# Five prices and waits of a list schedule: loads, stores and two gathers

## The chip, the core and the metric

One core of a Trainium2 chip runs the kernel. Its engines are TensorE (PE in the profile; its weight loads are PEld), VectorE (DVE), ScalarE (ACT) and GpSimd (POOL). SyncE (SP) computes nothing and issues most DMA transfers; GpSimd issues the rest. Each engine takes its instructions in the order in which the program gives them, and waits at the head of that order until the inputs and the buffer of the next one are there. The metric is device time in microseconds (us), the median of runs.

## The reference

The output of windowed attention goes through a routed layer of eight experts and then through a dense layer:

```python
# 2 x 8 heads, 576 tokens, 64 per head; window of 64
scores = where(0 <= i - j < 64, q @ k.T / 8, -1e9)
x = softmax(scores) @ v                     # as 1152 tokens x 512
logits = x @ w_gate                         # 8 experts, the best one per token
gate = softmax(logits)[best]
# tokens of one expert in order, at most 288 each
y[token] = gate * (relu(x[token] @ w1[best]) @ w2[best])   # 512 -> 1024 -> 512
h = y @ w_in                                # 512 -> 2048
out = (h * clip(h + 3, 0, 6) / 6) @ w_out   # 2048 -> 512
```

## The kernel before

**Attention.** The 1152 tokens lie in nine pairs of 64-token groups: pair j holds groups 2j and 2j+1. Per pair SyncE loads rows of q, k and v (`load_rows`, L472), TensorE turns them, and copies on VectorE or ScalarE bring them back from PSUM. `scores` (L564) multiplies, `mask_max` (L580, VectorE, line L587, four instructions) masks a group and finds its maxima, `exps` (L595, ScalarE, L600) takes the exponentials, `p_turn` (L606, TensorE, L610) turns them, `values` (L621, TensorE, L628) multiplies them with v and, in the same matmuls, with v times the gate's weights, so that the logits come along. `finish` (L637, VectorE) divides by the sums and `store_x` (L658, SyncE) stores the pair to DRAM.

**Routing and the early expert.** After five pairs the choice of experts for their tokens is made (`choose`, first row L125). The expert with the most of these tokens is the early expert: its weights are loaded (`early_load`), a gate step on VectorE works out flags and factors, five products on GpSimd (L897) prepare the tokens' index, and `early_gather` (L810) has GpSimd fetch 128 of its rows from DRAM. `early_scale` (L814) multiplies these rows by their gates, on ScalarE (line L468) or VectorE (L464); `early_turn` (L817) turns them, and TensorE starts on that expert. After the last pair `ranks` counts all tokens per expert and sorts the experts; its last line is the cast of the expert list (eofI, L948), from which SyncE takes the addresses of all the other experts' weights. `first_gather` (L965) then fetches the first rows for them.

**What sets the order in the attention.** A list scheduler, `run_nodes` (L430), writes the program. Each step is a node with a priority, the engines that can do it with a cost in us (PE, A, V, P, and D for SyncE's queue), the steps that it needs, the ring of buffers that it takes from, and a lag between its end on the engine and its result. The planner keeps a clock per engine (L406) and takes again and again the ready node with the lowest key

```python
t = max(clock[e], r)
if e == "PE" and t < COLD:
    c = 2 * c
key = (t + EPS * prio + (c if len(engs) > 1 else min(engs.values())) * CW, prio)
```

so a changed cost or lag moves steps on all engines: where a copy can run on ScalarE or VectorE, it also decides on which. Before COLD a TensorE step counts twice its cost.

**What sets it behind the attention.** A second planner writes the experts' stage. It starts from the clocks at which the first one ended (`est.update(clock)`, L1873), and from the planned ends of `rk` (the ranks) and `g0` (the first gather). Weights of an expert arrive in pieces of 512 KB (w1 at L280, w2 at L283) in a ring of buffers (raw); each half of a piece is split into a high part (a cast, L267, mostly on ScalarE) and a low part (L272, VectorE), and TensorE multiplies with both. TensorE's work goes into `fill` (L1263), which puts in front of it whatever job of SyncE, ScalarE, VectorE and GpSimd fits the planned time.

Among these jobs is the conversion of the dense layer's weights, which come as 64-bit numbers. A conversion job (`conv64`, L186; `conv_job`, L1147) loads 512 KB into one of three buffers (raw64, `NR64` = 3; L196 for w_in, L199 for w_out), takes an absolute value on ScalarE (L206), goes through five or six steps on VectorE (L212 to L236; the last one, L236, frees the buffer), and for the first units GpSimd stores the result to DRAM in 256 KB transfers. SyncE has one queue for all of this: an experts' load behind a conversion load leaves after it, even if its own buffer has long been free.

Of the kernel before, what the change touches and what calls it, by code (L numbers as in the profile page):

```python
# [23 lines left out]
def tile_kernel(ctx, tc, q, k, v, w_gate, w1, w2, w_in, w_out, out, cap):  # L24
    nc = tc.nc
    B, H, S, D = q.shape
# [82 lines left out]
    V = nc.vector  # L109
# [8 lines left out]
    def bc(ap, shape):  # L118
        return ap.to_broadcast(shape)
# [201 lines left out]

    NWARM = 9
    GAP = -0.2
    EPS, CW, COLD, LAG = 0.015, 0.3, 6.0, 0.15
    PRIO = {'q': -30, 'k': -29, 'v': -27, 'tq': -7, 'eq': 8, 'tk': -10, 'ek': 3, 'cv': 1, 'tv': 1, 'ev': 2, 'gw': 1, 'ew': 1, 'tw': 1, 'ex': -4, 's': 2, 'm': 5, 'e': 2, 'pt': 2, 'ep': 9, 'av': 2, 'f': 8, 'st': 0, 'top': -5, 'tail': 2, 'ear': 78, 'hot': 60, 'gt': 25, 'fl': 13, 'ga': 58, 'xE': 5, 'turn': 20}
    CS = {'xE': 1.15, 'ep': 1.07, 'eq': 1.07, 'sE': 1.15, 'rk': 1.3, 'q': 1.15, 'v': 0.7}
    with ExitStack() as actx:
# [64 lines left out]
        def rows(t, src, j):  # L392
            o = 0
            while o < 128:
                b, s = divmod(128 * j + o, S)
                n = min(128 - o, S - s)
                yield t[o : o + n, :, 0:D], src[b, :, s : s + n, :].rearrange("h p d -> p h d")
                o += n
# [4 lines left out]
        rings = {'q': 3, 'k': 4, 'v': 3, 'qd': NQD, 't': 2, 's': 2, 'sp': 1, 'p': 1, 'o': 1, 'x': 1, 'neg': 4, 'pe': 3, 'pT': 4, 'vT': 3, 'vw': 4, 'xt': 4}  # L403
        taken = {r: [] for r in rings}
        freed = {}
        clock = dict.fromkeys(("PE", "A", "V", "P", "D"), 0.0)  # L406

        def node(name, prio, engs, fn, needs=(), take=None, free=(), lag=LAG):
            engs = {e: c * CS.get(name[0] if isinstance(name, tuple) else name, 1.0) for e, c in engs.items()}
            nodes[name] = (prio, engs, fn, needs, take, free, lag)  # L410
# [61 lines left out]
        def load_rows(which, j):  # L472
            src, eng = {"q": (q, nc.sync), "k": (k, nc.sync), "v": (v, nc.sync)}[which]

            def run(e):
                box[which, j] = t = ld.tile([128, H, D], F32, name=which + "_sb", bufs=rings[which])
                for o, i in rows(t, src, j):
                    eng.dma_start(o, i)  # L478

            return run  # L480
# [24 lines left out]
        def turn_rows(src, key):  # L505
            def run(e):
                box[key] = pt = quarters(bank("t"))
                t = box[src]
                for hp in range(H // 2):
                    nc.tensor.transpose(  # L510
                        pt[:, hp, :], t[:, 2 * hp : 2 * hp + 2, :].rearrange("p h d -> p (h d)"), ident
                    )

            return run

        def q_out(j):
            def run(e):
                copy(e, qd[j % NQD], box["tq", j], D ** -0.5)

            return run  # L520

        def k_out(j):
            o = 64 * (j + 1)
            return lambda e: copy(
                e, kT[:, :, 0 : 2 * KO].rearrange("p h (a t) -> p h a t", a=2)[:, :, :, o : o + 64],
                box["tk", j].rearrange("p h (a t) -> p h a t", a=2),
            )
# [130 lines left out]
        def store_x(j):  # L658
            xt = box["xt", j]
            nc.sync.dma_start(x_dram[128 * j : 128 * j + 128, :], xt.rearrange("p a h d -> p (a h d)"))  # L660
# [10 lines left out]
        for j in range(NJ):  # L671
            p = 10 * j + (PRIO["tail"] if j == NJ - 1 else 0)
            for nm in ("q", "k", "v"):
                node(("l" + nm, j), p + PRIO[nm], {"D": 1.25}, load_rows(nm, j), take=nm, lag=2.0)
            parts = 3 if j + 1 < NJ else 2
            holders["v", ("lv", j)] = 1 + parts
            node(("tq", j), p + PRIO["tq"], {"PE": 0.44}, turn_rows(("q", j), ("tq", j)), [("lq", j)], "t", [("q", ("lq", j))])
            node(("eq", j), p + PRIO["eq"], {"A": 0.5, "V": 0.6}, q_out(j), [("tq", j)], "qd", [("t", ("tq", j))])
            node(("tk", j), p + PRIO["tk"], {"PE": 0.44}, turn_rows(("k", j), ("tk", j)), [("lk", j)], "t", [("k", ("lk", j))])
            node(("ek", j), p + PRIO["ek"], A_V, k_out(j), [("tk", j)], None, [("t", ("tk", j))])  # L680
            for i in range(parts):
                old = j - NV + (i == 2)
                node(
                    (f"cv{i}", j), p + PRIO["cv"] + i, {"P": 0.6}, v_copy(j, i), [("lv", j)] + [("av", old)] * (old >= 0),
                    None, [("v", ("lv", j))],
                )
            node(("tv", j), p + PRIO["tv"], {"PE": 0.44}, turn_rows(("v", j), ("tv", j)), [("lv", j)], "t", [("v", ("lv", j))])
            node(("ev", j), p + PRIO["ev"], A_V, v_out(j), [("tv", j)], "vT", [("t", ("tv", j))])
            node(("gw", j), p + PRIO["gw"], {"PE": 0.27}, v_gate(j), [("ev", j), "wg"], "x", [("vT", ("ev", j))])
            node(("ew", j), p + PRIO["ew"], {"A": 0.16, "V": 0.2}, w_out_(j), [("gw", j)], "vw", [("x", ("gw", j))])  # L690
            node(("tw", j), p + PRIO["tw"], {"PE": 0.11}, w_turn(j), [("ew", j)], "x", [("vw", ("ew", j))])
            old = [("av", i) for i in (j - NV, j - NV + 1) if i >= 0]
            node(("ex", j), p + PRIO["ex"], {"A": 0.32, "V": 0.4}, x_out(j), [("tw", j)] + old, None, [("x", ("tw", j))])
            for g in (2 * j, 2 * j + 1):
                o = p + g % 2
                if g % 2 == 0:
                    needs = [("eq", j), ("ek", j)] + [("ek", j - 1)] * (j > 0)
                    node(("s", j), o + PRIO["s"], {"PE": 0.93}, scores(j), needs, "sp", [("qd", ("eq", j))])
                    holders["sp", ("s", j)] = 2
                node(("m", g), o + PRIO["m"], {"V": 0.84}, mask_max(g), [("s", j)], "neg", [("sp", ("s", j))])  # L700
                node(("e", g), o + PRIO["e"], {"A": 1.17}, exps(g), [("m", g)], "pe", [("neg", ("m", g))])
                tp = "p" if g + 1 < NG else "t"
                node(("pt", g), o + PRIO["pt"], {"PE": 0.44}, p_turn(g), [("e", g)], tp, [("pe", ("e", g))])
                node(("ep", g), o + PRIO["ep"], A_V, p_out(g), [("pt", g)], "pT", [(tp, ("pt", g))])
            free = [("pT", ("ep", 2 * j)), ("pT", ("ep", 2 * j + 1))]
            needs = [("ep", 2 * j), ("ep", 2 * j + 1), ("ex", j), ("cv0", j), ("cv1", j)]
            if j:
                needs += [("ex", j - 1), ("cv2", j - 1)]
            node(("av", j), p + PRIO["av"], {"PE": 1.15}, values(j), needs, "o", free)
            if j + 1 < NJ:  # L710
                node(("f", j), p + PRIO["f"], {"V": 1.3}, lambda e, j=j: finish(j), [("av", j)], "xt", [("o", ("av", j))])
                node(("st", j), p + PRIO["st"], {"D": 0.62}, lambda e, j=j: store_x(j), [("f", j)], None, [("xt", ("f", j))])
            else:
                node(("f", j), p + PRIO["f"], {"V": 0.85}, lambda e, j=j: finish(j), [("av", j)])


        p = 10 * NE + PRIO["top"]
# [104 lines left out]
        def early_load(u, h):  # L822
            def run(e):
                if "eE" not in box:
                    box["eE"] = nc.sync.value_load(eI[0:1, 0:1], min_val=0, max_val=E - 1)
                weights_in(wE[2 * u + h], box["eE"], u, h)

            return run
# [55 lines left out]
        node("gE", p + PRIO["fl"], {"V": 1.35}, early_gate, ["fl"])  # L884
        node("ix", p + PRIO["fl"], {"PE": 0.2}, early_index, ["gE"], "x")
        node("ie", p + PRIO["fl"], {"V": 0.3}, early_index_out, ["ix"], None, [("x", "ix")])
        node("ga", p + PRIO["ga"], {"P": 1.04}, early_gather, ["ie"], lag=3.0)
        node("sE", p + PRIO["turn"], {"A": 0.48, "V": 0.4}, early_scale, ["ga"])
        node("tE", p + PRIO["turn"], {"PE": 0.44}, early_turn, ["sE"], "x")
        node(  # L890
# [3 lines left out]
        for j in range(NE):  # L894
            node(
                ("hotp", j), p + PRIO["hot"], {"P": 0.36},
                lambda e, j=j: nc.gpsimd.tensor_tensor(  # L897
                    out=A1t[:, j], in0=A1[:, j], in1=bc(c_tok[:, j : j + 1], [128, 128]), op=ALU.mult
                ),
                ["gE"],  # L900
            )
        for u in range(NFU):
            for h in range(2):
                node(("wl", u, h), p + 2 * u + h, {"D": 1.3}, early_load(u, h), ["pl"], lag=2.0)
        for u in range(NEU):
            o = p + PRIO["ear"] + 2 * u
            node(("e0", u), o, {"PE": 0.86}, early_up(u, 0), ["xE", ("wl", u, 0)], "s")
# [88 lines left out]
        p = -100  # L996
# [4 lines left out]
        node("sa", p, {"V": 1.4}, slots, ["rk"], None, [("t", "cn")])  # L1001
        node("px", p, {"PE": 0.25}, slot_index, ["sa"] + [("hotp", j) for j in range(NE)], "t")
        node("sx", p, {"V": 0.1}, lambda e: V.tensor_copy(sidx, box["ix"][:, 0:NA]), ["px"], None, [("t", "px")])
        node("g0", p, {"P": 1.04}, first_gather, ["sx"], lag=3.0)
        node("gt", PRIO["gt"], {"V": 0.9}, gate_parts, ["ch"])
        node("gc", PRIO["gt"], {"V": 0.6}, gate_columns, ["gt", "px"])
        for j in range(NE, NJ):
# [46 lines left out]
    for n, (small, b) in enumerate(TEAMS):  # L1054
        at_ = dict.fromkeys("abw", 0)
        order = ORDER[n]
        for c in order:
            f = at_[c]
# [795 lines left out]
    for g, (small, b) in enumerate(TEAMS):  # L1854
        st = start[False, small[0]]
# [134 lines left out]
```

## Time and profile before

| what | before |
|---|---|
| median of 3 runs | 445.79 us |
| lowest to highest | 444.71 to 446.35 us |
| the profiled execution's own time | 445.48 us |
| its span in the trace | 443.7 us |
| mean granted clock of TensorE | 0.983 |
| TensorE busy | 410.0 us, 92% |
| VectorE busy | 322.7 us, 73% |
| ScalarE busy | 224.8 us, 51% |
| GpSimd busy | 56.7 us, 13% |

The trace covers the span; 1.8 us of the profiled execution's time lie outside it. Attention and routing take the first 75 us or so; the experts follow, from 238 us on mixed with the dense layer (the first ScalarE step of its gate, L1556, starts at 237.5), which fills the rest. Shares over the whole span say little of one stage, so the prediction reads single stretches: a table by stage (busy time, granted clock and DMA share in a stretch), the chain of waits (followed back from the last instruction, each step to what released it) and timelines of one engine (when each instruction started, and in brackets how long the engine had been idle and for whom).

### The profile page before, as it was taken

What the parts mean: (1) busy time and instruction counts of PE and PEld (TensorE: products, weight loads), DVE (VectorE), ACT (ScalarE), POOL (GpSimd) and SP (SyncE); (2) the same over time, 40 slices, a digit from 0 to 9 for tenths busy, and PEclk for the clock granted to TensorE, in tenths of its full rate; (3) what the DMA queues carried; (4) which work ended last, traced back from release to release, by engine and by line L of the source; (5) the groups of instructions that cost most, each with busy time, mean ns of one, the idle gap of its engine ahead of it and who ended that gap; (6) DMA issues with size and microseconds to landing.
All of it is one profiled execution on the core that took longest, in us unless ns stands there. A gap on an engine that the chain in (4) does not pass through costs nothing.

```text
span 443.7 us, 8561 instructions
## 1 busy us (share of the span) xinstructions
PE 410.0 (92%) x3055; PEld 348.2 (78%) x3055; DVE 322.7 (73%) x867; ACT 224.8 (51%) x492; POOL 56.7 (13%) x120
## 2 busy tenths in 40 slices
PE   7999867699698999999899999999999999999992
PEld 4887654488587898987689998888888888998981
DVE  2888937779799999979777999999999422222430
ACT  4886733572458877735468453455553222322330
POOL 8632401203002002010000000000000000110111
PEclk9999989999899999999899999999999999999997
DMA  9996943996999999569975323442410000110101
GB/s 173 202 234 159 323 153 114 341 338 199 369 338 364 328 324 353 169 171 381 354 234 192 100 90 100 139 124 71 134 55 0 1 0 0 49 47 1 47 28 51
DMA packets 68883, 75.99 MB, mean 171 GB/s; under 512 B 31104, under 2 KB 49536, under 8 KB 68832
## 3 DMA queue, kind: packets, MB, share of 16 engines
q1 hardware_dynamic: 66288, 67.13, 49.6%
q0 software_dynamic: 2544, 8.23, 4.9%
q8 instruction: 26, 0.43, 0.4%
q14 instruction: 25, 0.20, 0.2%
HBM read 67.49 MB, written 7.86 MB: 170 GB/s over the span
## 4 chain that ended last, share of the span: by engine, by line
PE 64%; DVE 14%; DMA 13%; ACT 3%; issue 3%; SPq 2%; POOL 0%; POOLq 0%; DVEq 0%; ACTq 0%
PE banks L253 54%; DMA raw<-in_moe_w_dram 9%; DVE wt L272 5%; PE banks L628 2%; PE banks L510 2%; DMA c<-x_dram,eI 2%; PE banks L610 1%; ACT wt L267 1%; DMA v_sb<-in_v_dram 1%; SPq L478 1%; PE banks L574 1%; PE banks L1495 1%; DMA out_dram<-part,cidx 1%; DVE neg L587 1%; DVE raw L221 1%
## 5 line engine op out<-in xcount | busy, mean ns | idle before, releaser
L253 PE MATMUL banks<-x,wt 128*128 128x320 f32 (+3 forms) x576 | 107.2, 336 | 0.5 <-ACT x L1386 0.4
L253 PEld LDWEIGHTS banks<-x,wt 128*128 128x128 f32 x576 | 94.3, 188 | 10.7 <-DVE wt L272 0.7
L253 PE MATMUL banks<-wt,g 128*128 128x512 f32 x384 | 92.8, 390 | 0.0
L272 DVE TENSOR_TENSOR wt<-raw,wt 128x512 fp32r<-128x512 f32 x128 | 82.5, 684 | 11.6 <-ACT wt L267 10.7
L267 ACT CAST wt<-raw 128x512 fp32r<-128x512 f32 x128 | 75.3, 621 | 30.7 <-DMA raw<-in_moe_w_dram 21.1
L253 PEld LDWEIGHTS banks<-wt,g 128*128 128x128 f32 x384 | 71.6, 188 | 14.2
L1556 ACT ACTIVATE r<-banks,c_three 128x320 f32<-128x320 f32 (+3 forms) x48 | 27.9, 581 | 70.3 <-PE banks L253 70.3
L1559 DVE SCALAR_TENSOR_TENSOR gf<-r,banks 128x320 f32<-128x320 f32 (+3 forms) x48 | 26.5, 552 | 47.7 <-ACT r L1556 47.3
L253 PE MATMUL banks<-xT,wt 128*128 128x256 f32 (+2 forms) x288 | 39.9, 286 | 2.3 <-ACT wt L267 1.5
L253 PEld LDWEIGHTS banks<-xT,wt 128*128 128x128 f32 x288 | 35.7, 194 | 4.8 <-ACT wt L267 2.3
L253 PE MATMUL banks<-h,wt 128*128 128x256 f32 (+2 forms) x288 | 37.0, 279 | 0.0
L253 PEld LDWEIGHTS banks<-h,wt 128*128 128x128 f32 x288 | 34.6, 191 | 0.5 <-issue 0.5
L1562 ACT CAST g<-gf 128x320 fp32r<-128x320 f32 (+2 forms) x40 | 21.4, 536 | 21.0 <-DVE gf L1559 20.8
L1565 DVE TENSOR_TENSOR g<-gf,g 128x320 fp32r<-128x320 f32 (+2 forms) x40 | 23.3, 582 | 9.5 <-ACT g L1562 9.1
L253 PE MATMUL banks<-wt,xT 128*128 128x256 f32 x144 | 22.8, 305 | 4.8 <-ACT wt L267 3.4
L206 ACT ACTIVATE c<-raw 128x512 f32<-128x512 f32 x32 | 21.5, 675 | 10.6 <-DVE t L230 10.1
L253 PEld LDWEIGHTS banks<-wt,xT 128*128 128x128 f32 x144 | 19.8, 201 | 7.6 <-ACT wt L267 4.6
L1602 POOL DMA_INDIRECT out_dram<-raw,cidx x4 | 4.0, 988 | 160.7 <-issue 158.1
L587 DVE CUSTOM_DVE_ANT_0 neg<-banks,tmask 128x128 f32<-128x128 f32 x72 | 16.3, 284 | 8.7 <-PE banks L574 8.7
L600 ACT ACTIVATE pe<-neg,nmx 128x128 f32<-128x128 f32 x72 | 22.4, 392 | 0.1
L230 DVE SCALAR_TENSOR_TENSOR t<-raw,c 128x512 f32<-128x512 uint32 x32 | 22.0, 687 | 0.7 <-DMA wd_dram<-t 0.2
L221 DVE SCALAR_TENSOR_TENSOR raw<-raw,c 128x512 uint32<-128x512 uint32 x32 | 22.0, 687 | 0.3
(286 smaller groups left out, 568.2 us busy)
## 6 DMA issues: line engine op xcount, KB each, us to landing
raw<-in_moe_w_dram SPq DMA_DIRECT2D x64, 512.0 KB
raw<-in_moe_w_in_dram SPq DMA_DIRECT2D x16, 512.0 KB
raw<-in_moe_w_out_dram SPq DMA_DIRECT2D x16, 512.0 KB
early<-in_moe_w_dram SPq DMA_DIRECT2D x8, 512.0 KB
wd_dram<-t POOLq DMA_DIRECT2D x12, 256.0 KB, 5.9
raw<-wd_dram SPq DMA_DIRECT2D x6, 512.0 KB
x_dram<-xt SPq DMA_DIRECT2D x9, 256.0 KB
q_sb<-in_q_dram SPq DMA_DIRECT2D x8, 256.0 KB
```

Of the source, the lines that this page charges most:

```text
L206: nc.scalar.activation(box["c"].bitcast(F32), box["hi"].bitcast(F32), AF.Abs)
L221: nc.vector.scalar_tensor_tensor(out=a.bitcast(U32), in0=box["hi"], scalar=0xC0000000, in1=box["c"], op0=ALU.bitwise_and, op1=ALU.bitwise_or,)
L230: nc.vector.scalar_tensor_tensor(out=box["t"], in0=box["lo"], scalar=2.0 ** -52, in1=box["c"].bitcast(F32), op0=ALU.mult, op1=ALU.mult)
L253: nc.tensor.matmul(out, l, r, start=(start and n == 0), stop=(stop and n == len(pairs) - 1))
L267: nc.scalar.copy(hi, r)
L272: V.tensor_tensor(out=lo, in0=r, in1=hi.bitcast(F32), op=ALU.subtract)
L587: V.tensor_tensor_reduce(out=neg[:, hp, :], in0=box["sp", g][:, hp, :], in1=tmask[:, first, :], scale=-1.0, scalar=3.0e38, op0=ALU.add, op ...
L600: nc.scalar.activation(pe[:, hp, :], neg[:, hp, :], AF.Exp, bias=nmx[:, hp : hp + 1], scale=-1.0)
L1556: nc.scalar.activation(r, ph, AF.Relu, bias=c_three)
L1559: V.scalar_tensor_tensor(out=gf, in0=r, scalar=6.0, in1=ph, op0=ALU.min, op1=ALU.mult)
L1562: nc.scalar.copy(hi, gf)
L1565: V.tensor_tensor(out=lo, in0=gf, in1=hi.bitcast(F32), op=ALU.subtract)
```

## The change

Seven numbers of the two planners' inputs are changed, all in the attention's list schedule. A load of q, k, v counts 1.46 us of SyncE's queue in place of 1.25, a store of a pair 0.73 in place of 0.62, a load of the early expert's weights 1.46 in place of 1.3. The queue's clock starts at 2.4 in place of 0, and TensorE's steps count double until 8.4 in place of 6.0. The early expert's gather counts as landed 6 us after its issue in place of 3, the first gather of the experts' stage 5 in place of 3.

```diff
@@ -321,7 +321,7 @@
-    EPS, CW, COLD, LAG = 0.015, 0.3, 6.0, 0.15
+    EPS, CW, COLD, LAG = 0.015, 0.3, 8.4, 0.15
@@ -403,7 +403,7 @@
-        clock = dict.fromkeys(("PE", "A", "V", "P", "D"), 0.0)
+        clock = dict.fromkeys(("PE", "A", "V", "P"), 0.0) | {"D": 2.4}
@@ -671,7 +671,7 @@
-                node(("l" + nm, j), p + PRIO[nm], {"D": 1.25}, load_rows(nm, j), take=nm, lag=2.0)
+                node(("l" + nm, j), p + PRIO[nm], {"D": 1.46}, load_rows(nm, j), take=nm, lag=2.0)
@@ -709,7 +709,7 @@
-                node(("st", j), p + PRIO["st"], {"D": 0.62}, lambda e, j=j: store_x(j), [("f", j)], None, [("xt", ("f", j))])
+                node(("st", j), p + PRIO["st"], {"D": 0.73}, lambda e, j=j: store_x(j), [("f", j)], None, [("xt", ("f", j))])
@@ -884,7 +884,7 @@
-        node("ga", p + PRIO["ga"], {"P": 1.04}, early_gather, ["ie"], lag=3.0)
+        node("ga", p + PRIO["ga"], {"P": 1.04}, early_gather, ["ie"], lag=6.0)
@@ -901,7 +901,7 @@
-                node(("wl", u, h), p + 2 * u + h, {"D": 1.3}, early_load(u, h), ["pl"], lag=2.0)
+                node(("wl", u, h), p + 2 * u + h, {"D": 1.46}, early_load(u, h), ["pl"], lag=2.0)
@@ -1001,7 +1001,7 @@
-        node("g0", p, {"P": 1.04}, first_gather, ["sx"], lag=3.0)
+        node("g0", p, {"P": 1.04}, first_gather, ["sx"], lag=5.0)
```

What is computed and every instruction's shape stay as they are. The order changes in the attention, and, because the second planner starts from the first one's clocks, in the experts' stage up to about 205 us of the trace of before; behind that the order is the same.

On ScalarE, before, the scaling of the early expert's gathered rows (L468) stands ahead of the exponentials (L600) of group 16, the first group of the last pair (pe); pT are turned exponentials, vx and vy copies of v with gates, L848 and L648 the last steps of the attention:

```order
L600 ACTIVATE pe<-neg,nmx 128x128 x4
L468 ACTIVATE c_1184<-c_1184,sgE 128x512
L600 ACTIVATE pe<-neg,nmx 128x128 x4
L466 COPY pT<-banks 128x512
L600 ACTIVATE pe<-neg,nmx 128x128 x4
L466 COPY pT<-banks 128x512
L848 ACTIVATE t_1331<-banks 128x256
L648 ACTIVATE xt<-banks,rd 128x64 x8
```

and after (the same place, from the copy ahead of the exponentials of groups 14 and 15):

```order
L466 COPY pT<-banks 128x512
L600 ACTIVATE pe<-neg,nmx 128x128 x8
L466 COPY pT<-banks 128x512 x2
L600 ACTIVATE pe<-neg,nmx 128x128 x8
L466 COPY pT<-banks 128x512 x2
L466 COPY early<-banks 128x512
L648 ACTIVATE xt<-banks,rd 128x64 x8
```

There is no scaling on ScalarE any more: exponentials and their copies follow each other up to the copy of the turned rows (early) and the last pair's division (L648).

On VectorE, after, between the finish of pair 7 (L643 to L656, xt being the finished rows) and that of pair 8 (from L640; rd are reciprocals of the sums, lv the logits' parts):

```order
L655 TENSOR_TENSOR xt<-banks,rd 128x512
L656 TENSOR_REDUCE logits<-lv 128x8
L464 TENSOR_SCALAR c_1194<-c_1194,sgE 128x512
L640 TENSOR_SCALAR rd<-banks 128x8
L641 RECIPROCAL rd<-rd 128x8
L643 TENSOR_TENSOR lv<-banks,rd 128x64
L656 TENSOR_REDUCE logits<-lv 128x8
```

The scaling (L464) is here now, behind pair 7 and ahead of pair 8.

On SyncE, before, in the experts' stage; L280 and L283 are loads of an expert's w1 and w2 (the ISA row reads the expert's number), L199 is the fourth conversion load, of w_out; the first load left at 93.8 us, the second at 103.1:

```order
L280 DMA raw_1715<-in_moe_w1_dram 128x4x256
L199 DMA raw64_1774<-in_moe2_w_out_dram 128x1024
L283 ISA
L283 DMA raw_1805<-in_moe_w2_dram 128x2x512
L280 ISA
L280 DMA raw_1807<-in_moe_w1_dram 128x4x256
```

and after:

```order
L280 DMA raw_1719<-in_moe_w1_dram 128x4x256
L199 DMA raw64_1757<-in_moe2_w_out_dram 128x1024
L196 DMA raw64_1800<-in_moe2_w_in_dram 128x2x512
L283 ISA
L283 DMA raw_1808<-in_moe_w2_dram 128x2x512
L280 ISA
L280 DMA raw_1810<-in_moe_w1_dram 128x4x256
```

A fifth conversion load (L196, of w_in) now stands behind the fourth, ahead of the expert's w2 that followed it directly.

## Rows read from the trace of the kernel before

**Rows 1.** Table by stage: busy us of each engine, granted clock, DMA share.

```profile
core 0: us, PE busy (x) PEld busy (x) DVE busy (x) ACT busy (x) POOL busy (x), PEclk, DMA share, GB/s
40.00:60.00 20.00, 13.96 (x240) 10.74 (x240) 16.18 (x117) 13.80 (x42) 5.22 (x10) 1.00 0.82 271
60.00:65.00 5.00, 5.00 (x46) 4.55 (x47) 2.90 (x14) 2.18 (x7) 0.00 (x0) 0.67 0.14 54
100.00:105.00 5.00, 5.00 (x44) 4.79 (x44) 4.83 (x11) 0.81 (x3) 1.29 (x2) 1.00 0.23 25
110.00:115.00 5.00, 1.80 (x16) 1.57 (x14) 2.81 (x8) 1.14 (x3) 0.58 (x1) 0.95 1.06 353
115.00:120.00 5.00, 4.86 (x26) 3.87 (x26) 4.13 (x8) 4.00 (x9) 0.00 (x0) 0.71 1.06 378
180.00:200.00 20.00, 20.00 (x176) 17.98 (x176) 17.51 (x42) 10.25 (x24) 1.15 (x2) 1.00 0.55 156
```

**Rows 2.** Chain of waits: start us, us, what; 30 to 120 us.

```profile
51.34 7.16 DMA c<-x_dram,eI
...
59.96 2.15 PE banks L628 x32
62.10 1.05 PE banks L610 x4
...
66.33 1.20 PE banks L628 x32
...
76.33 7.90 DMA raw<-in_moe_w_dram
...
106.13 11.54 DMA raw<-in_moe_w_dram
```

**Rows 3.** Timeline of GpSimd: start us, us, engine, line, operation.

```profile
49.34 1.82 POOL L897 TENSOR_TENSOR A1t<-A,c_tok 128x128 f16<-128x128 f16 x5
51.34 1.20 POOL L805 DMA_INDIRECT c<-x_dram,eI  x1 [0.18 <-DVE nmx L587]
```

**Rows 4.** Timeline of ScalarE; in brackets the idle time and its releaser.

```profile
58.53 0.72 ACT L468 ACTIVATE c<-c,sgE 128x512 f32<-128x512 f32 x1 [3.39 <-DMA c<-x_dram,eI]
59.15 1.27 ACT L600 ACTIVATE pe<-neg,nmx 128x128 f32<-128x128 f32 x4
...
114.25 1.14 ACT L267 CAST wt<-raw 128x512 fp32r<-128x512 f32 x2 [3.66 <-DMA raw<-in_moe_w_dram]
```

**Rows 5.** Timeline of VectorE in four stretches.

```profile
38.38 0.20 DVE L125 TENSOR_REDUCE top_m<-logits 128x5 f32<-128x40 f32 x1
...
42.68 0.28 DVE L587 CUSTOM_DVE_ANT_0 neg<-banks,tmask 128x128 f32<-128x128 f32 x1
...
43.52 0.20 DVE L761 TENSOR_TENSOR top_f<-oh,subE 128x40 f32<-128x40 bf16 x1
...
48.01 0.21 DVE L462 COPY vx<-banks 128x64 f32<-128x64 f32 x1
...
48.64 0.69 DVE L462 COPY pT<-banks 128x512 f32<-128x512 f32 x1
...
50.91 0.28 DVE L587 CUSTOM_DVE_ANT_0 neg<-banks,tmask 128x128 f32<-128x128 f32 x1
...
71.75 0.17 DVE L948 CAST eofI<-eofF 128x8 int32<-128x8 f32 x1
...
102.42 0.68 DVE L236 TENSOR_TENSOR t<-raw,t 128x512 f32<-128x512 f32 x1
...
105.68 0.69 DVE L236 TENSOR_TENSOR t<-raw,t 128x512 f32<-128x512 f32 x1
```

**Rows 6.** Timeline of SyncE's queue: when transfers were issued.

```profile
38.88 0.38 SPq L478 DMA_DIRECT2D v_sb<-in_v_dram  x1
...
103.13 0.34 SPq L199 DMA_DIRECT2D raw<-in_moe_w_out_dram  x1
103.71 0.38 SPq L283 DMA_DIRECT2D raw<-in_moe_w_dram  x1
```


## The prediction

> **What bounds the kernel now.** I read the table of stages first. From 40 to 60 us TensorE works 14.0 of 20 us and VectorE 16.2, and from 60 to 65 us TensorE's granted clock is 0.67, half its full level for most of that stretch [rows 1]. The chain of waits says why: it runs through one DMA, the gather of the early expert's rows, from 51.34 for 7.16 us, and then through the values step of pair 7, which takes 2.15 us where that of pair 8 takes 1.20 [rows 2]. So TensorE, VectorE and ScalarE stood still together for about 3.4 us, ScalarE because the scaling of the gathered rows stands in its order ahead of the exponentials of group 16 [rows 4], and the work behind it ran at 1.2 instead of 2.4 GHz for a while. Behind the attention the chain goes through loads of expert weights (76.33, 106.13) [rows 2]. They cannot leave before the routing's expert list, the cast at 71.75 [rows 5]. So an attention that ends its routing x us earlier lets the experts' loads start x us earlier.
>
> A second place matters: from 100 to 105 us the DMA engines are 0.23 busy while TensorE works without a gap, and from 110 to 115 us TensorE works only 1.8 of 5 us, with a clock of 0.71 behind that [rows 1]. SyncE had sat before a load of the second weights (at 103.13), whose buffer a conversion on VectorE frees (102.42, 0.68 us); the expert's load behind it left at 103.71 [rows 5, 6], and ScalarE waited 3.66 us for weights until 114.25 [rows 4].
>
> **The change, part by part.** No instruction is added, removed or resized. All of it is order, and two products of the order count.
>
> The loads' new price and start only shift the planner's clocks. On SyncE they bring the stores of finished pairs one to three places forward, ahead of loads, and a store waits for its pair on VectorE, so loads behind it leave later. The last load of v left at 38.88 [rows 6]; behind the new fifth store it leaves when pair 4 is done, by my walk at about 43, and lands before 48. I cost that at nothing: the first VectorE step that needs it stands at about 54 in the new order. If the cover were gone, every us beyond that would count.
>
> First term, the attention. I walked the new order by hand, each engine taking its next step when inputs and buffers are there, with the old trace's durations. The early part gets worse: pair 3 is finished at about 35.7, and ahead of pair 4's finish VectorE now has two mask steps (42.68 to 43.52 is one, 0.84), a three-part copy (48.01 to 48.64, 0.63) and three copies of 0.6 [rows 5]: 35.7 + 4.1 + 0.8 for two waits on TensorE + 1.5 for the finish gives the choice of experts (first row at 38.38) a start at 42.2, 3.8 later. From there VectorE hardly waits. Before, 38.38 to 50.91 is 12.5 us without a gap [rows 5]; the new order leaves two mask steps and a three-part copy out of that stretch (2.3) and puts one scaling copy in (0.6): 10.8. Then four mask steps (3.4), two finishes (2.7) and two small copies (0.7) follow up to the finish of pair 7: 17.6, plus 1.2 for two waits, ends at 61.0. The gather starts later too: the five products on GpSimd (49.34, 1.82 us) follow VectorE's gate step at 52.2, so it starts at 54.3, and with its old 7.2 us lands at 61.5 [rows 3, 4]. Scaling on VectorE (0.45), latency and four transposes (0.7) let the values of pair 8 start at 62.6, where they started at 66.33 [rows 2]. In this order the exponentials, turns and values of pairs 7 and 8 no longer stand behind the scaling, TensorE has no gap of 3 us, and I take the full clock. From those values to the cast of the expert list it was 5.4 us (66.33 to 71.75) [rows 2, 5] and stays so. **Term one: -3.6.** Bounds: -4.6, if the gather lands so early that only the last turn holds the values back; -1.0, if the walk is 1 us off and the half clock, worth 1.6 to 2 us (2.15 against 1.20, 1.05 for two turns against half of it [rows 2]), comes all the same. I take -3.6 since the same walk over the old order meets the old times within 0.6 up to the gather.
>
> What the Trainium skill says would speak another way on the gather. The row shows 7.2 us from its start to the scaling [rows 4]. The page DMA: Bandwidth & Descriptors, section Queues, rings and completion order, says that each DMA engine takes its queues in turn, packet by packet, so a gather from GpSimd need not wait for weights queued by SyncE; its section Anatomy of one DMA fits 2.0 us plus the bytes at 436 GB/s, an estimate of 2.6 us behind the issue of 1.2. By that the rows would be there at 58.1, before VectorE is free, and the sum would be lower by 0.6. The trace does not agree; I keep the row.
>
> Second term, the experts' queue. The new planner moves one more load for the conversion of the second weights ahead of an expert's load, where SyncE sat at 103.13. That load needs the buffer of the second conversion, whose last step began at 105.68 and took 0.69 [rows 5]. So the expert's load that left at 103.71 [rows 6] now leaves at 106.4 + 0.6 less the 3.3 us (term one at that place, two copies of ScalarE having changed places) = 103.7, as before: at this one place the whole gain is lost. In front of it in the queue lies one 512 KB load, as before; but about two transfers of 256 KB from GpSimd's queue are now out earlier, in a gap, each 0.7 us at 353 GB/s [rows 1]. So the weights of 114.25 come at 112.8, not at 110.7: +2.1. Behind it the fifth conversion load is missing from the queue (512 KB at 353 to 378 GB/s is 1.4), and TensorE has a few waits to take that back in; I count 0.7 of it. **Term two: +1.4.** Bounds: 0, if the queue holds enough transfers to cover the stall, and +3.6, if nothing is taken back.
>
> Third, the conversions run up to one piece (four to five VectorE steps, some 2 us) further ahead between 125 and 200 us and level off at 205. I cost that at nothing: VectorE has 2.5 us idle from 180 to 200 us [rows 1] and the total is the same. Without that cover it costs up to 1.6. Everything after 205 is in the old order.
>
> **Sum.** 445.48 is the profiled execution's own time, 0.3 below the median of the three runs (445.79): 445.48 - 3.6 + 1.4 = 443.3. Half a per cent is 2.2 us, about what a measurement of this kernel can tell from no change: below 443.6 is faster, above 448.0 slower.
>
> **Rivals.** *The whole gain survives*: the queue's other transfers cover SyncE's longer stall. For it: the DMA share is 1.06 from 110 to 120 us, so bytes decide there [rows 1]; against: 0.23 just before. 445.48 - 3.6 = 441.9. *Slower*: the moved conversion load is what decides. Place: SyncE behind 103.13. If the queue is empty when the expert's load leaves, TensorE waits the whole distance between the two conversions, 105.68 - 102.42 = 3.3, and the moved load's own 1.4, and the conversion steps now ahead of the experts' scalings on VectorE cost their 1.6, since VectorE is busy 4.8 of 5 us from 100 to 105 [rows 1, 5]: 445.48 - 3.6 + 6.3 = 448.2. It decides from the point where that load leaves later than 103.7. *The plan is still wrong about the gather*: the planner now counts 7.0 us, the trace 7.2, and the weights of the early expert still run beside it. Scaling and transposes stand ahead of the finish and values of pair 8, so beyond 61.5 each us costs one, and a wait over 3 us may bring the half clock back: at 9.5 us for the gather 445.48 - 3.6 + 2.3 + 1.4 = 445.6, with the half clock 447.3; I put 446.0. By the page above it has no chance; by the row some.
>
> **Chances.** Forecast 0.42, its own range 441.8 to 444.8; the whole gain 0.17; the conversion load 0.24; the gather late 0.17. Just over half of the forecast and nearly all of the second lie below 443.6; more than half of the third lies above 448.0. So faster 0.42, same 0.38, slower 0.20. The range takes in the second case, most of the third and the bounds of term one: 440.3 to 448.3.
>
> **What would show it.** Right: no gap over 1.5 us on the three engines between 50 and 62 us, the clock at 1.0 from 60 to 65 us, the scaling on VectorE, the cast of the expert list at 68.2 (term one); the expert's load behind the fifth conversion load still near 103.7 and the weights' wait on ScalarE ending near 112.8 with a wait on TensorE of over 3.2 us before it (term two); no gap in TensorE's work from 180 to 200 us (third). Wrong: a cast after 70.5, a scaling that waits for the gather past 62.5, or loads of the experts that leave 3 us earlier at that place.

## The result and the profile after

| kernel | median of runs | ratio to before, 95% interval | profiled execution, span |
|---|---|---|---|
| before | 445.25 us | | 445.48, 443.7 |
| changed | 452.39 us (451.03 to 453.23) | 1.0145 (1.0105 to 1.0184) | 452.90, 451.2 |

(The median before is of four runs here, of three ahead of the prediction.) The changed kernel is 7.1 us slower, outside the range of the prediction and on the other side of no change. The work is the same: TensorE has 3055 matmul records in both traces. It is 413.5 us busy where it was 410.0, at a mean granted clock of 0.976 in place of 0.983, so of the 7.5 us that the span grew some 4.0 went into waits of TensorE and some 3.5 into matmuls that ran slower. Where the time went is read by looking up the same group of matmuls in both chains of waits. Before (start us, us, what):

```profile
98.70 4.50 PE banks L253 x36
...
190.99 4.30 PE banks L253 x36
...
206.44 8.47 DMA raw<-in_moe_w_dram
...
230.85 3.35 PE banks L253 x30
```

After, with the last values steps of the attention ahead of them:

```profile
56.70 2.15 PE banks L628 x32
...
66.40 1.20 PE banks L628 x32
...
102.85 4.50 PE banks L253 x36
...
113.98 9.90 DMA raw<-in_moe_w_dram
...
202.01 4.30 PE banks L253 x36
...
208.00 7.90 DMA raw<-in_moe_w_dram
...
238.77 3.35 PE banks L253 x30
```

The values of pair 8 start at 66.40, where they started at 66.33 [rows 2]: in these two executions the attention neither gained nor lost. At the first group of 36 matmuls the changed kernel is 4.2 us behind, at the second 11.0, and 7.9 at the group of 30. (Between these two groups both kernels wait for weights, which landed at 214.9 before and 215.9 after; the changed kernel has more of TensorE's work left behind that wait, 22.9 us up to the group of 30 against 15.9.) So the loss lies in the experts' stage, between 75 and 200 us. TensorE's own timeline shows it as three waits (idle us and releaser in brackets). After:

```profile
88.19 1.09 PE L1306 MATMUL banks<-ident,xg 128*128 128x128 f32 x4 [3.12 <-issue]
...
121.74 3.02 PE L253 MATMUL banks<-wt,xT 128*128 128x256 f32 x12 [5.87 <-ACT wt L267]
...
161.24 1.67 PE L253 MATMUL banks<-wt,h 128*128 128x512 f32 x6 [3.15 <-ACT h L1436]
```

The same groups before:

```profile
84.53 0.63 PE L1306 MATMUL banks<-ident,xg 128*128 128x128 f32 x4 [0.32 <-PE banks L859]
...
114.92 3.02 PE L253 MATMUL banks<-wt,xT 128*128 128x256 f32 x12 [3.20 <-ACT wt L267]
...
151.09 1.66 PE L253 MATMUL banks<-wt,h 128*128 128x512 f32 x6 [0.45 <-ACT h L1436]
```

**First wait.** ScalarE after, then VectorE after:

```profile
85.75 0.62 ACT L267 CAST wt<-raw 128x512 fp32r<-128x512 f32 x1 [2.69 <-DMA raw<-in_moe_w_dram]
86.27 0.58 ACT L1309 CAST xT<-banks 128x512 fp32r<-128x512 f32 x1
```

```profile
86.40 0.69 DVE L272 TENSOR_TENSOR wt<-raw,wt 128x512 fp32r<-128x512 f32 x1 [2.62 <-ACT wt L267]
87.01 0.68 DVE L1312 TENSOR_TENSOR xT<-banks,xT 128x512 fp32r<-128x512 f32 x1
87.61 0.48 DVE L1298 TENSOR_SCALAR xg<-xg,sgate 128x512 f32<-128x512 f32 x1
```

A cast of weights (L267) that waits for its transfer until 85.75 stands on ScalarE ahead of the cast of the first gathered rows (L1309). Its split (L272) stands on VectorE ahead of the scaling of the next rows (L1298), and TensorE needs these to turn them at 88.19. The profile puts the wait down to "issue"; the rows behind it were done at 88.1, which is what ended it. Before, two casts and two splits fewer stood ahead of these rows. **Second and third wait**, SyncE after:

```profile
106.33 0.34 SPq L199 DMA_DIRECT2D raw<-in_moe_w_out_dram  x1
109.90 0.37 SPq L196 DMA_DIRECT2D raw<-in_moe_w_in_dram  x1
110.53 0.91 SPq L283 DMA_DIRECT2D raw<-in_moe_w_dram  x1
...
140.33 0.37 SPq L280 DMA_DIRECT2D raw<-in_moe_w_dram  x1
148.98 0.38 SPq L196 DMA_DIRECT2D raw<-in_moe_w_in_dram  x1
150.20 0.37 SPq L283 DMA_DIRECT2D raw<-in_moe_w_dram  x1
```

The expert's load behind the fifth conversion load left at 110.53, not at 103.71 as before [rows 6]. The ninth conversion load, which the prediction does not mention, had moved ahead too: SyncE sat before it until 148.98, the expert's load behind it left at 150.20. What both loads waited for are VectorE's last steps of earlier conversions, which free the buffers:

```profile
109.18 0.69 DVE L236 TENSOR_TENSOR t<-raw,t 128x512 f32<-128x512 f32 x1
...
148.27 0.68 DVE L236 TENSOR_TENSOR t<-raw,t 128x512 f32<-128x512 f32 x1
```

The table of stages after has the prices (busy us, granted clock, DMA share):

```profile
40.00:60.00 20.00, 16.78 (x244) 12.70 (x240) 16.26 (x100) 11.59 (x36) 6.78 (x12) 0.85 0.79 233
60.00:65.00 5.00, 4.60 (x76) 3.58 (x75) 3.82 (x23) 3.53 (x11) 0.00 (x0) 0.93 0.96 312
...
88.00:91.00 3.00, 2.81 (x7) 1.81 (x8) 2.17 (x5) 0.58 (x1) 0.00 (x0) 0.50 1.07 364
100.00:105.00 5.00, 5.00 (x44) 4.30 (x43) 4.90 (x15) 2.79 (x7) 0.00 (x0) 1.00 0.00 0
...
141.00:149.00 8.00, 5.41 (x37) 4.57 (x36) 7.57 (x16) 6.15 (x13) 0.00 (x0) 1.00 0.58 197
```

From 100 to 105 us, where the DMA engines were 0.23 busy before [rows 1], they now stand still, and from 141 to 149 they are 0.58 busy while TensorE works 5.4 of 8 us. The wait of 3.1 us at 85 us brought half the clock behind it (0.50 from 88 to 91). In the changed kernel's attention the clock is 0.85 over 40 to 60 us and 0.93 from 60 to 65, where it was 1.00 and 0.67 [rows 1]: half clock came earlier, and for longer.

### The profile page after: what moved, and what is told of

Same layout as the page of the kernel before. It is cut to its first block, busy times and chain, and to the rows that moved or that the text cites. A ratio compares the mean times of both kernels' runs of the same rounds, so it can differ in the third digit from the quotient of the medians.

```text
span 451.2 us, 8575 instructions
## 1 busy us (share of the span) xinstructions
PE 413.5 (92%) x3055; PEld 349.4 (77%) x3055; DVE 323.9 (72%) x860; ACT 224.9 (50%) x499; POOL 57.3 (13%) x120
## 4 chain that ended last, share of the span: by engine, by line
PE 67%; DVE 11%; DMA 10%; ACT 4%; issue 4%; SPq 1%; POOL 0%; POOLq 0%; ACTq 0%; DVEq 0%
PE banks L253 55%; DMA raw<-in_moe_w_dram 8%; DVE wt L272 4%; PE banks L628 2%; PE banks L510 2%; PE banks L610 2%; PE banks L574 2%; DMA c<-x_dram,sidx 2%; ACT wt L267 1%; PE banks L1470 1%; PE banks L667 1%; ACT pe L600 1%; PE banks L540 1%; SPq L283 0%; PE banks L1306 0%
## 5 line engine op out<-in xcount | busy, mean ns | idle before, releaser
L272 DVE TENSOR_TENSOR wt<-raw,wt 128x512 fp32r<-128x512 f32 x128 | 83.2, 687 | 18.8 <-ACT wt L267 18.1
L267 ACT CAST wt<-raw 128x512 fp32r<-128x512 f32 x128 | 75.0, 619 | 31.5 <-DMA raw<-in_moe_w_dram 22.6
L253 PE MATMUL banks<-xT,wt 128*128 128x256 f32 (+2 forms) x288 | 38.7, 283 | 2.6 <-DVE wt L272 2.2
L600 ACT ACTIVATE pe<-neg,nmx 128x128 f32<-128x128 f32 x72 | 22.7, 392 | 0.9 <-DVE nmx L587 0.8
L253 PE MATMUL banks<-wt,h 128*128 128x512 f32 x72 | 19.6, 406 | 3.8 <-ACT h L1436 3.8
```

What stands on the lines that cost most here:

```text
L253: nc.tensor.matmul(out, l, r, start=(start and n == 0), stop=(stop and n == len(pairs) - 1))
L267: nc.scalar.copy(hi, r)
L272: V.tensor_tensor(out=lo, in0=r, in1=hi.bitcast(F32), op=ALU.subtract)
L600: nc.scalar.activation(pe[:, hp, :], neg[:, hp, :], AF.Exp, bias=nmx[:, hp : hp + 1], scale=-1.0)
```

## The experiments

Two theories were set against each other. A: the loss sits in the order of the experts' stage. B: it sits in the attention. Since the second planner knows the first only by its end clocks, the two stages can be taken apart by writing these clocks in as constants. A kernel's ratio is to the kernel before on the same chip (its medians there were 445.2 to 446.0 us), in brackets its 95% interval; differences between kernels in us are between medians.

**The two stages apart.** `oldatt_newseed` is the kernel before with the clocks that the changed attention planned, `newatt_oldseed` the changed kernel with the old ones:

```diff
+    clock.update({'PE': 74.392, 'A': 71.592, 'V': 72.922, 'P': 70.962, 'D': 60.624})
+    done['rk'], done['g0'] = 67.722, 75.962
+    for u, (a, b) in enumerate(zip([50.342, 53.262, 56.182, 59.102], [51.802, 54.722, 57.642, 61.292])):
+        done['wl', u, 0], done['wl', u, 1] = a, b
     est.update(clock)
```

For `newatt_oldseed` the numbers are 67.914, 62.854, 68.314, 66.354, 55.249 for the clocks, 63.114 and 69.354 for ranks and first gather.

> The attention in the order of before, the experts' stage in the order of after: the planner of the experts' stage is started from the clocks, the ranks' end, the first gather's and the early weights' ends that the changed attention planned, written in as constants. Theory A (the loss of the changed kernel sits in the experts' order: casts of weights ahead of the gathered rows on ScalarE, conversion loads ahead of experts' loads on SyncE): most of the 7 us come with this kernel alone, 449 to 453 us. Theory B (the loss sits in the attention, in the half clock from 54 to 61 us and in the early expert's matmuls that now come after the last values step): 445 to 447 us.

Measured: 452.88 us, 1.0151 (1.0096 to 1.0205).

> The attention in the order of after, the experts' stage in the order of before (started from the clocks that the old attention planned, as constants). Theory A: 444 to 447 us, the attention by itself costs or gains at most 1.5 us, since the expert list is cast at 71.83 us in both traces within 0.1. Theory B: 449 us or more.

Measured: 443.10 us, 0.9943 (0.9916 to 0.9971). Theory B falls. The order of the experts' stage alone, with not one attention instruction moved, makes the kernel as slow as the whole change, and its trace has the same three waits of TensorE (2.7, 6.0 and 4.5 us). The new attention alone makes it 2.3 to 2.5 us faster, more than the 1.5 that Theory A allowed. The two do not simply add: under the new experts' order the new attention is worth 0.5 us (452.88 to 452.39), which is not clear of noise.

**The first gather's lag.** `g0only` and `nog0` change `lag=3.0` of `first_gather` to 5.0 in the kernel before, and back to 3.0 in the changed one.

> Of the seven numbers only the lag of the first gather, 3 to 5. It puts one more cast and one more split of weights ahead of the first gathered rows on ScalarE and VectorE and changes nothing of SyncE's order. If such a cast is what makes TensorE wait at 85 us, since it waits for weights that are still on their way: 1 to 3 us slower than before, 446.5 to 448.5 us. If ScalarE's order there has slack: same as before.

Measured: 445.79 us, 1.0018 (0.9979 to 1.0056): no change.

> The changed kernel with the first gather's lag back at 3. SyncE's order stays that of the changed kernel; on ScalarE and VectorE the casts still stand ahead of the first rows, only one scaling changes places. Theory A with SyncE's queue as the main part: no more than 0.5 us from the changed kernel, 451.5 to 453 us. If the lag of the first gather is the main part: 448 us or less.

Measured: 451.88 us, 1.0131 (1.0082 to 1.0180), 0.5 below the changed kernel. What this number costs here is not clear of the noise: one more cast ahead of the first rows can be borne.

**Three moves put back.** The next four keep the changed kernel's plan and hold single instructions back when the program is written. `fifth_late` and `ninth_late` keep a conversion load until so many experts' loads were written:

```diff
-            load()
+            conv_n[0] += 1
+            if held:
+                flush()
+            if conv_n[0] in HELD_N:      # {5: 6} or {9: 18}
+                held.append([load, HELD_N[conv_n[0]]])
+            else:
+                load()
```

`rows_first` holds casts and splits back:

```diff
-            high(e)
+            put("h", lambda: high(e))    # at most 5 until the first rows' L1309
...
-            box["low"]()
+            put("l", box["low"])         # at most 2 until the first L1298, 5 until the second
```

> The changed kernel, its plan kept, with two casts and their splits given to ScalarE and VectorE behind the first gathered rows of the experts' stage instead of ahead of them, as before. Theory A1 (the casts ahead of the rows, which wait for weights until 85.75 us, make TensorE stand 3.1 us at 85 us and run at half clock to 91): TensorE reaches its first experts' weights some 3 to 4 us earlier, and the time falls by 1.5 to 4 us against the changed kernel, to 448.5 to 451 us. Theory A2 (SyncE's conversion loads decide behind that anyway): the gain is taken back, 451.5 us or more.

Measured: 450.35 us, 1.0089 (1.0057 to 1.0121). TensorE's wait is gone, by its timeline:

```profile
83.02 0.63 PE L1323 MATMUL banks<-ident,xg 128*128 128x128 f32 x4 [0.24 <-PE banks L859]
```

(L1323 is L1306 here.) The move is worth 2.0 us by the medians; the intervals of the ratios of this and the changed kernel overlap, so the size is rough. (The group starts 5.2 us earlier than in the changed kernel's trace; 2.0 of that come from the attention, whose expert list is cast at 69.85 in this execution, at 71.83 in the changed kernel's.)

> The changed kernel, its plan kept, with one SyncE instruction moved: the fifth conversion load is issued behind six loads of experts' weights, as before, instead of ahead of them. This is the second term of the prediction by itself. If it is worth what the prediction took (1.4, at most 3.6): 449 to 451 us. If the stall of 5.9 us on TensorE near 115 to 121 us goes back to 3.2 and nothing takes it back, -2.5: 449.9 us. If other conversion loads stall as much behind it: same as the changed kernel.

Measured: 449.43 us, 1.0091 (1.0054 to 1.0128), 3.0 below the changed kernel, by intervals that overlap a little as well. TensorE's second wait went from 5.87 to 1.96:

```profile
113.26 3.02 PE L253 MATMUL banks<-wt,xT 128*128 128x256 f32 x12 [1.96 <-ACT wt L267]
```

> The changed kernel, its plan kept, with one SyncE instruction moved: the ninth conversion load, before which SyncE sat from 140.7 to 149.0 us with the DMA engines idle, is issued behind eighteen more loads of experts' weights, as before. Theory A3 (this load is the largest single part of the loss): 446 to 449 us. If the weights that it holds up are needed late enough, or the wait comes back at 208 us: 451 us or more.

Measured: 447.57 us, 1.0034 (0.9989 to 1.0078): one DMA issue, moved behind 18 experts' loads on SyncE, is worth 4.8 us, and here the intervals do not overlap. From 150 to 160 us TensorE worked 8.08 us in the changed kernel and works 9.64 here:

```profile
140.00:150.00 10.00, 8.32 (x62) 6.91 (x61) 9.73 (x20) 8.75 (x19) 1.71 (x3) 1.00 0.98 326
150.00:160.00 10.00, 9.64 (x77) 9.18 (x76) 9.39 (x22) 8.18 (x19) 2.42 (x2) 1.00 0.89 290
```

> The three moves together on the changed kernel, its plan kept otherwise. If they are the whole loss of the experts' stage: 442 to 445 us, as with the old attention's seeds (443.1). If the rest of the order (casts and conversion steps on ScalarE and VectorE, the seventh and eighth conversion load) carries some of it: 446 to 449 us.

Measured: 443.88 us, 0.9960 (0.9929 to 0.9990). The three together give back 8.5 us (9.8 as a sum of the three apart) and end within 0.8 of the new attention with the old experts' order. They are the loss within what the noise can tell; the casts and conversion steps that stay in their new places cost nothing that shows.

**Which number does what.** With the experts' stage held at the old clocks, `gaonly_oldseed` has the early gather's lag of 6 alone, `queue_oldseed` the five numbers of the queue and the cold start without either gather's lag, `load_oldseed` the lag of 6 and the loads' 1.46.

> Of the seven numbers only the lag of the early expert's gather, 3 to 6, and the experts' stage kept in the order of before (its planner started from the old clocks, as constants). If the attention's gain comes from the gather alone, it has the whole gain of the new attention, 2 to 2.5 us, or more, since the choice of experts then isn't delayed by the new order of the loads: 441 to 443 us. If the new prices of the loads and stores carry it: 445 us, same as before.

Measured: 438.99 us, 0.9846 (0.9801 to 0.9890), the fastest of all and below the 441 to 443 that was expected: 6.8 below before, 13.4 below the changed kernel.

> Of the seven numbers the five of SyncE's queue and the cold start (loads, stores, early weights, the queue's start, COLD), not the two lags of gathers, and the experts' stage kept in the order of before (old clocks as constants). In the changed kernel's trace the choice of experts starts 4.1 us later (42.49 against 38.38 us); if these five numbers do that and the gather's stall stays: slower than before, 446 to 449 us. If they are free, as the prediction costed them: 445 to 446 us.

Measured: 447.04 us, 1.0036 (1.0003 to 1.0068), slower by some 1.6, with an interval that nearly reaches no change.

> The early gather's lag of 6 and the price of the q, k and v loads of 1.46, the experts' stage in the order of before (old clocks as constants). By the order, the price of the loads alone puts two mask steps ahead of the fifth pair's finish on VectorE. If that is what costs the attention its gain: the choice of experts starts near 42 us, 442.5 to 444 us. If another of the prices does it: 439 to 440 us.

Measured: 439.34 us, 0.9846 (0.9813 to 0.9878). The second case came true: the loads' price does bring the choice of experts to 41.7 us, but costs next to nothing, so another price takes the attention's gain. The cast of the expert list, first in `gaonly_oldseed`, then in `load_oldseed`, then in `newatt_oldseed`:

```profile
65.71 0.17 DVE L948 CAST eofI<-eofF 128x8 int32<-128x8 f32 x1
```

```profile
66.83 0.17 DVE L948 CAST eofI<-eofF 128x8 int32<-128x8 f32 x1
```

```profile
70.83 0.17 DVE L948 CAST eofI<-eofF 128x8 int32<-128x8 f32 x1
```

`load_oldseed` and `newatt_oldseed` differ by the start, COLD, the early weights' price and the stores' 0.73. By the programs' order only the stores' price matters among these: all seven new numbers but that one give, with the old clocks, the order of `load_oldseed` word for word on every engine. So the two runs differ in order by the stores' price alone, and it makes the last 4 us (439.34 to 443.10; the intervals do not overlap). It does so only on top of the loads' price: with the gather's lag and without the loads' price, the stores' price leaves the order of `gaonly_oldseed` as it is. In the traces the values of pair 6 (first L628 of 32) start at 50.7 us with the loads' price, and at 56.3 with both, behind the product with the early expert's index instead of ahead of it, and at half the clock; the values of pairs 7 and 8 come as much later.

**The clock.** `busy_gaps` is `newatt_oldseed` with five matmuls of zeros where TensorE waits between 48 and 54 us:

```diff
+        def idle(t, n):
+            for _ in range(n):
+                nc.tensor.matmul(t[:, 0:512], warm[:, 0:128], warm, start=True, stop=True)
```

> The new attention with the experts' stage of before, and five small matmuls of zeros more on TensorE, put where it waited between 48 and 54 us (one ahead of a turn of gates, two ahead of the turn of group 12, two ahead of the early expert's index product), into banks that are overwritten right behind them. The new attention ran at half clock from 52 to 59 us after such waits. If the waits are what brings the half clock, and this is enough work: clock 1.0 there, the expert list cast 1 to 2 us before 70.8, 441 to 442 us. If not enough: half clock as before, 443 to 444 us.

Measured: 443.69 us, 0.9955 (0.9920 to 0.9990). The stages of `newatt_oldseed`:

```profile
48.00:52.00 4.00, 2.53 (x21) 1.47 (x25) 4.00 (x30) 3.87 (x13) 1.22 (x2) 1.00 0.59 195
52.00:56.00 4.00, 3.17 (x45) 2.35 (x39) 3.62 (x24) 0.73 (x3) 3.08 (x6) 0.51 0.99 327
56.00:60.00 4.00, 4.00 (x69) 3.44 (x65) 2.16 (x15) 3.26 (x10) 0.06 (x1) 0.63 1.07 377
```

and of `busy_gaps`:

```profile
48.00:52.00 4.00, 3.37 (x26) 1.92 (x26) 4.00 (x32) 3.57 (x11) 1.22 (x2) 1.00 0.52 168
52.00:56.00 4.00, 3.02 (x51) 1.88 (x51) 3.97 (x28) 1.50 (x6) 2.54 (x6) 1.00 0.97 333
56.00:60.00 4.00, 3.96 (x83) 3.09 (x77) 3.36 (x23) 3.25 (x11) 0.60 (x1) 1.00 1.06 371
```

The clock stays at its full level and the expert list is cast at 69.78, 1.05 earlier, but the time does not differ from that of `newatt_oldseed` within the intervals. One execution doesn't show that the five matmuls did it: of the seven kept traces with this attention and no matmul more, six were at half clock somewhere between 52 and 60 us and cast the list at 70.59 to 72.08, but the seventh, `rows_first`, kept the full clock and cast at 69.85. The clock of the other executions speaks for the matmuls: its mean over the run was 0.986 or more in ten of the twelve of `busy_gaps` and in three of the ten of `newatt_oldseed`. Yet those three took 443.0 to 443.2 us and the other seven 441.6 to 444.9. So the half clock in the attention goes with a cast of the expert list that is 0.7 to 2.2 us later; in the whole time nothing of it shows here.

**The lag alone, nothing held.**

> Of the seven numbers only the lag of the early expert's gather, 3 to 6, and nothing pinned: the experts' planner starts from the clocks of this attention. Its conversion loads then stand as in the changed kernel (the fifth and the ninth early). If that lag both frees the attention and spoils the experts' order: 439.0 and the 7 to 9 us that this order cost, 446 to 448 us, and slower by some 7 to 8 us than the same attention with the old clocks. If an attention that ends 6 us earlier takes the experts' order without loss: 441 us or less.

Measured: 445.92 us, 1.0003 (0.9971 to 1.0036). The attention ends as early as in `gaonly_oldseed` (cast at 65.70), and the experts' stage gives all of it back, by the same three waits as in the changed kernel:

```profile
79.91 0.63 PE L1306 MATMUL banks<-ident,xg 128*128 128x128 f32 x4 [1.68 <-issue]
112.40 3.02 PE L253 MATMUL banks<-wt,xT 128*128 128x256 f32 x12 [6.39 <-ACT wt L267]
...
151.67 2.93 PE L253 MATMUL banks<-wt,h 128*128 128x512 f32 x6 [3.80 <-ACT h L1436]
```

So the whole of the change in short: the early gather's lag gains 6.8 us in the attention; the prices of loads and stores give back some 4 of them; and the clocks with which the attention hands over, 4 to 9 us later in the plan than before though the ranks end no later on the chip, cost some 9 in the experts' stage (443.10 to 452.39; with the old attention 7.5, with the lag alone 6.9). Which of the handed clocks does it was not tried.

## Why the prediction was wrong, point by point

**Term one, the attention, -3.6 (-4.6 to -1.0): right in its mechanism, too large.** By itself it is -2.3 to -2.5. The prediction's own sign spoke against it: the expert list was to be cast at 68.2 (62.6 + 5.4 would be 68.0), a cast after 70.5 was to mean "wrong", and it came at 71.83, in `newatt_oldseed` at 70.83. There the cast is only 0.9 earlier than before, while that execution is 1.8 shorter (443.71 against 445.48): part of the gain lies behind the routing, and no run shows where. The gap behind the gather is gone, the scaling sits on VectorE, behind the finish of pair 7, and no longer waits:

```profile
65.04 0.26 DVE L656 TENSOR_REDUCE logits<-lv 128x8 f32<-128x64 f32 x1
65.22 0.47 DVE L464 TENSOR_SCALAR c<-c,sgE 128x512 f32<-128x512 f32 x1
```

The gather took 7.2 us again, as the DMA view after shows (us from issue to landing):

```profile
c<-x_dram,eI POOLq DMA_INDIRECT x1, 7.2
```

The issue itself took 1.2 of these, so 6.0 lie behind it. That speaks, as in the old trace, against the 2.6 us behind the issue that I had estimated from the Trainium skill, DMA: Bandwidth & Descriptors, section Anatomy of one DMA. The walk was good to within 1 us up to the gather: choice of experts at 42.2 forecast, 42.49 measured; five products at 52.2 and 52.48; gather at 54.3 and 55.24. It failed behind it. I let VectorE's steps set the pace with 1.2 us of waits up to the finish of pair 7 at 61.0. It ended at 65.3, because there the pace is TensorE's: turns, values of pair 6, scores and turns follow each other from 55.02 on, and TensorE was at half clock, the values of pair 6 taking 2.15 as those of pair 7 did before. With the full clock (`rows_first`) the values of pair 8 start at 64.42, still 1.8 later than the forecast 62.6. "I take the full clock" is the other part of the miss: half clock was a bound of mine, and I tied it to a gap of 3 us; here waits of 0.4 to 1.1 us went ahead of it.

**Loads and stores, costed at nothing: wrong.** I looked at when the last load of v lands, and that was covered. But the prices also moved TensorE's and VectorE's order: the values of pair 6 went behind the index product. The stores' price on top of the loads' does that (some 4 us), and the lag alone shows what the attention could have had (-6.8).

**Term two, the fifth conversion load, +1.4 (0 to 3.6): right place, half the size.** Its own price is some 3.0. The load behind it left at 110.53, forecast was 103.7. The forecast had the distance between two conversions in it, 3.3, and set term one's gain of 3.3 against it. The distance came nearly as forecast (106.33 to 109.90, 3.6). The gain did not: by the forecast the fourth conversion load would have left at 99.8 (103.13 less 3.3), and it left at 106.33. Of these 6.5 us, 3.3 are the gain that this attention did not bring and 3.2 a delay that the stage already had. Nothing took the loss back, as in the upper bound of 3.6: the DMA engines had nothing left to move from 100 to 105.

**Third term, conversions further ahead, cost nothing: the step that failed.** I compared VectorE's work with its idle time and saw that the order levels off at 205 us. The conversions' loads were not followed through SyncE's queue there. The ninth load moved 18 experts' loads ahead, to where its buffer was not free before 148.98: 4.8 us in place of nothing, the largest single part of the miss. The prediction asked for exactly this at the fifth load, and not at the others.

**Not in the prediction at all:** the two casts that moved ahead of the first rows, 2.0 us.

The forecast was 443.3, the result 452.4, so 9.1 us are missing. Priced apart, the parts give 1.3 (term one), 1.6 (term two), 4.8 (the ninth load) and 2.0 (the casts), 9.7 in all; together they weigh a little less.

The rival "slower" named the right mechanism, a conversion load that blocks SyncE, and 448.2 us; with the ninth load counted like the fifth (another 3.3 for the distance of two conversions and 1.4 for the load, by that rival's own working) it would have come to 452.9. That this is so near the result is partly luck: it takes -3.6 for an attention that is worth -2.3, 4.7 for a fifth load that costs 3.0 and 1.6 for conversion steps that cost nothing that shows, and it lacks the 2.0 of the casts.

## What to carry to other kernels

When one planner hands its clocks to another, a truer number in the first is a change of the second's input: print both orders, and follow every load that moved through its queue, to what frees its buffer, not only the first one. A load whose buffer comes free late holds up all that is queued behind it; put it behind the loads whose buffers are free, since one such instruction was worth 4.8 us here. And try the numbers one by one: the gather's lag alone, with the experts' order kept, was worth 1.5%, and it was hidden under the six others.

## What the runs showed of the hardware

TensorE's clock fell to half without one long gap. In `newatt_oldseed` it worked 2.53 of 4 us from 48 to 52 us, in waits of 0.4 to 0.6, and was at 0.51 from 52 on; in `rows_first`, whose attention has the same order, it worked 2.99 and then 2.27 of 4 us and stayed at 1.00. So one order of instructions shows either in different executions. And the gather of 128 rows took 6.9 to 7.5 us from issue to landing in the thirteen kept traces that show it, whether anything waited for it or not.
